# The last stage of an attention and gated feed-forward kernel as fifteen block products instead of seven, with some block sums made by adding transfers

## The chip, the cores and the metric

The kernel runs on one core of a Trainium2 chip. The metric is the device time of the program in microseconds (us). The core has a matrix engine (TensorE, PE in the rows; PEld is its weight load), a vector engine (DVE), a scalar engine (ACT), GpSimd (POOL) and a sync engine (SP) that issues most transfers; 16 DMA engines move the data. Each engine works through its own list of instructions in order, and waits where one of them needs something that isn't there yet.

## The reference

Eight sequences of 576 tokens with eight heads go through windowed attention. Its output is the input x of a gated feed-forward layer with 4608 tokens, 512 model channels and 1536 inner channels:

```
scores = where(mask, q @ k^T / 8 + bias, -1e9);  attn = softmax(scores)
x      = (attn @ v), heads put side by side            # [4608, 512]
hid    = sigmoid(x @ w_gate) * (x @ w_val)             # [4608, 1536]
out    = hid @ w_out                                   # [4608, 512]
```

This case is about the last line, out = hid @ w_out. In the kernel it is computed transposed: out^T, 512 rows by 4608 columns.

## The kernel before, in words

Three parts follow one another on the matrix engine: the attention (with the first feed-forward chunks beside it), then `ffn2`, which makes hid in chunks of 128 inner channels and writes them to DRAM, then `last`, which reads hid back and makes out. All three products of the feed-forward are in float32 quality: a value is split into a high part in the matrix engine's format (a cast) and the remainder (value minus high part, on the vector engine), and each product is three matmuls, high by high, high by remainder, remainder by high. A block of 128 by 1024 values costs one cast (scalar engine, or vector engine where the planner finds that better) and one subtraction of 1024 elements per partition on the vector engine. The function `parts` (lines 206 to 216 in its helpers `copy` and `minus`) issues the two.

`last` (called five times, from line 1068) works through five groups of columns, three of 2 x 512 and two of 2 x 384. In each group the product is cut 2 by 2 by 2: two halves of the output rows, two sets of six inner chunks, two halves of the columns. Seven block products, with sums of blocks ahead of them and sums of results behind them, take the place of eight. Block sums are made on the vector engine (line 881), results leave PSUM by the scalar engine (line 889) or are added there by the vector engine (line 892), and are stored by SP. The weight side of the seven products is made ahead by `prepare_o`, while `ffn2` runs: it decodes w_out, makes the sums, splits them into high part and remainder, and writes both to DRAM (`stash_o`). `fetch_o` reads them back into the places of the gate and value weights as `ffn2` gives these up. One product in a group is 36 matmuls: two row blocks, six inner chunks, three parts.

The split blocks ("duos", 128 x 1024, high part and remainder) lie in a ring of six buffers; a product uses three, so the next product can be prepared while one runs. The blocks of hid lie in fifteen places, twelve per group and three for sums.

The order of instructions on each engine is not written by hand: `Graph.order` plays the whole program with estimated costs (`dve_cost`, `act_cost`, transfer sizes over a rate) and each engine's list is the order that comes out. SP's list is one queue, in order: a load stands behind a store that waits for its result. For a vector instruction with two operands of 1024 elements `dve_cost` gives 1.13 us, for one that adds PSUM onto 512 elements 0.60 us.

## Time and profile before

| what | value |
|---|---|
| median of 3 runs | 962.1 us (962.04 to 962.5) |
| span of the profiled execution (the only time that its page gives) | 962.2 us |
| PE busy | 956.3 us, 99% |
| DVE busy | 763.7 us, 79% |
| ACT busy | 517.9 us, 54% |
| POOL busy | 143.7 us, 15% |
| moved by DMA | 186 MB, mean 193 GB/s, 56% of the 16 engines' time |

A row of the profile names an engine, a line of the kernel, the tile written and the tiles read, the shape, and the number of instructions; behind it stand the busy time, the mean of one instruction in ns, and how long the engine stood idle just before these instructions and for whom. Matmuls overlap, so that the mean ns of one is more than the time from one to the next. "Clock" is the TensorE clock that was granted, 1.00 being full speed.

### The profile page before, as it was taken

To read this page: it belongs to the slowest core of one execution; us is meant where nothing else is said; L and a number is where in the kernel's file an instruction comes from. 1 tells how busy PE (TensorE), PEld (TensorE's weight loads), DVE (VectorE), ACT (ScalarE), POOL (GpSimd) and SP (SyncE) were. 2 spreads that over 40 slices of the span, in tenths; PEclk is the share of its full clock that TensorE was granted. 3 is DMA by queue.
4 is the path that set the end of the run, shared out by engine and by line. 5 is a ranking of instruction groups with operands and counts; after the bars stand their busy time and mean duration, and the time that the engine had idled before them with its cause. 6 is when DMAs were issued, how large, how long until landed. Compare 5 with 4: busy or idle time off the path is not lost.

```text
span 962.2 us, 18740 instructions
## 1 busy us (share of the span) xinstructions
PE 956.3 (99%) x6648; PEld 834.5 (87%) x6648; DVE 763.7 (79%) x1893; ACT 517.9 (54%) x1341; POOL 143.7 (15%) x316
## 2 busy tenths in 40 slices
PE   8999999999999999999999999999999999999998
PEld 7778888888889999999988888888888888889998
DVE  7999788788898899878976775674598878878773
ACT  7998788878876354434533543443344433333341
POOL 3645345444441000000000000000000000000000
PEclk9999999999999999999999999999999999999999
DMA  8887678867654344335583483379856254352601
GB/s 295 274 280 256 223 266 291 282 203 241 232 198 162 122 147 138 104 143 191 179 287 113 159 284 132 143 284 347 317 189 204 103 166 163 94 167 91 189 25 50
DMA packets 82653, 186.03 MB, mean 193 GB/s; under 512 B 7808, under 2 KB 36864, under 8 KB 82560
## 3 DMA queue, kind: packets, MB, share of 16 engines
q1 hardware_dynamic: 82416, 184.71, 56.1%
q8 instruction: 52, 0.85, 0.4%
q14 instruction: 41, 0.34, 0.1%
q10 hardware_dynamic: 144, 0.13, 0.0%
HBM read 121.90 MB, written 62.91 MB: 192 GB/s over the span
## 4 chain that ended last, share of the span: by engine, by line
PE 98%; ACT 1%; DMA 1%; SPq 0%; DVE 0%; issue 0%; ACTq 0%
PE mm L795 42%; PE mm L929 27%; PE mm L661 14%; PE mm L461 5%; PE mm L532 4%; PE mm L575 3%; PE mm L613 2%; PE mm L292 1%; DMA early_ar<-in_q_dram 1%; ACT pb L490 0%; ACT early_h L207 0%; SPq L212 0%; DVE early_hs L680 0%; ACT cout L889 0%; ACT spread L207 0%
## 5 line engine op out<-in xcount | busy, mean ns | idle before, releaser
L795 PE MATMUL mm<-xc,w2s 128*128 128x384 f32 (+1 forms) x2016 | 404.0, 362 | 0.0
L795 PEld LDWEIGHTS mm<-xc,w2s 128*128 128x128 f32 x2016 | 363.7, 188 | 40.0 <-DVE later_hs L802 0.7
L929 PE MATMUL mm<-duo,wo 128*128 128x512 f32 (+1 forms) x1260 | 258.9, 367 | 0.0
L929 PEld LDWEIGHTS mm<-duo,wo 128*128 128x128 f32 x1260 | 229.3, 188 | 29.6
L661 PE MATMUL mm<-first,first 128*128 128x512 f32 x576 | 156.2, 407 | 0.1
L661 PEld LDWEIGHTS mm<-first,first 128*128 128x128 f32 x576 | 101.2, 188 | 21.3 <-issue 1.1
L806 ACT ACTIVATE sg<-mm 128x384 f32<-128x384 f32 (+1 forms) x96 | 52.2, 545 | 111.5 <-PE mm L795 63.3
L802 DVE TENSOR_TENSOR mm<-mm,low 128x384 f32<-128x384 f32 (+1 forms) x96 | 60.2, 628 | 61.1 <-PE mm L795 60.4
L207 ACT COPY low<-mm 128x512 f32<-128x512 f32 (+1 forms) x93 | 49.6, 536 | 77.8 <-PE mm L795 65.7
L490 ACT ACTIVATE pb<-pb,st 128x128 f32<-128x128 f32 x216 | 84.6, 398 | 2.0 <-DVE st L486 1.9
L586 POOL TENSOR_SCALAR_AFFINE_SELECT pt<-spread 128x384 f32<-128x384 f32 x96 | 53.1, 576 | 44.8 <-ACT spread L207 44.1
L586 POOL TENSOR_SCALAR_AFFINE_SELECT pt<-early_h 128x384 f32<-128x384 f32 x96 | 51.3, 553 | 56.4 <-ACT early_h L207 56.0
L478 DVE COPY_PREDICATED mm<-early_h,mm 128x256 f32<-128x256 int32 (+1 forms) x144 | 48.7, 388 | 5.8 <-PE mm L461 5.8
L532 PEld LDWEIGHTS mm<-pt,vr 64*64 64x64 f32 x1056 | 43.2, 133 | 10.0 <-issue 4.7
L486 DVE CUSTOM_DVE_ANT_0 pb<-mm,early_h 128x128 f32<-128x128 f32 x216 | 49.5, 281 | 0.0
L532 PE MATMUL mm<-pt,vr 64*64 64x192 f32 (+2 forms) x1056 | 47.3, 284 | 0.0
L568 DVE TENSOR_SCALAR pb<-pb,st 128x128 f32<-128x128 f32 x169 | 42.1, 295 | 1.3
L490 ACT ACTIVATION_READ_ACCUMULATOR pb<-pb,st 128x1 f32 x216 | 41.9, 194 | 0.0
L207 ACT CAST duo<-csum 128x1024 fp32r<-128x1024 f32 (+1 forms) x26 | 25.2, 970 | 30.2 <-PE mm L929 13.2
L810 DVE SCALAR_TENSOR_TENSOR later_hs<-sg,later_hs 128x384 f32<-128x384 f32 (+1 forms) x48 | 30.1, 626 | 13.8 <-ACT sg L806 13.6
L207 ACT COPY early_h<-mm 128x384 f32<-128x384 f32 (+3 forms) x75 | 32.1, 444 | 13.9 <-PE mm L532 8.7
L802 DVE TENSOR_TENSOR later_hs<-mm,later_hs 128x384 f32<-128x384 f32 (+1 forms) x48 | 29.7, 619 | 12.2 <-ACT sg L806 6.5
(144 smaller groups left out, 1204.9 us busy)
## 6 DMA issues: line engine op xcount, KB each, us to landing
hid<-later_hs SPq DMA_DIRECT2D x24, 512.0 KB, 3.4
wo<-stash_o SPq DMA_DIRECT2D x12, 896.0 KB, 7.6
vr<-in_v_dram SPq DMA_DIRECT2D x32, 288.0 KB, 4.7
hid<-later_hs SPq DMA_DIRECT2D x24, 384.0 KB, 2.9
stash_o<-wtmp SPq DMA_DIRECT2D x12, 768.0 KB, 3.9
wraw<-in_moe_w_gate_dram SPq DMA_DIRECT2D x14, 512.0 KB, 4.9
wraw<-in_moe_w_val_dram SPq DMA_DIRECT2D x14, 512.0 KB, 4.3
kr<-in_k_dram SPq DMA_DIRECT2D x11, 576.0 KB, 4.8
```

Of the source, the lines that this page charges most:

```text
L207: g.add("ACT", act_cost(n, psum), lambda: nc.scalar.copy(out(), src()), reads, writes, want, release=release, slack=slack, ways=[("DVE", d ...
L461: nc.tensor.matmul(to, qraw(u)[rows, i // 2, h * D:(h + 1) * D], keys, start=True, stop=True)
L478: g.add("DVE", dve_cost((a1 - a0) * P, psum=True), lambda b=b, a0=a0, a1=a1: nc.vector.copy_predicated(quads(b)[:, a0:a1, 1:3], before[:, ...
L486: g.add("DVE", 0.21, lambda: nc.vector.tensor_tensor_reduce(pb()[:, e], sp[b][:, a, D:D + P], relm[u.p][:, w], op0=ALU.add, op1=ALU.min, s ...
L490: g.add("ACT", 0.39, lambda: nc.scalar.activation(pb()[:, e], pb()[:, e], AF.Exp, bias=st()[:, e:e + 1], scale=-1.0, accum_out=st()[:, 3 + ...
L532: nc.tensor.matmul(mm[WORK[h]][e * D:(e + 1) * D, a - e * S - cuts[h]:b - e * S - cuts[h]], vraw(u)[r * D:r * D + D, c], seen, start=first ...
L586: nc.gpsimd.affine_select(pt(u)[:, f0:f0 + 2 * n - 1:2, :], both(), [[0, n], step], cmp, 0.0, base=0, channel_multiplier=mult)
L661: nc.tensor.matmul(mm[s][:, 0:wd], w.tile(kind, wi, i)[:, c * P:(c + 1) * P], xpart(x, c)[:, 0:wd], start=(k == 0 and c == 0), stop=(k == ...
L795: nc.tensor.matmul(mm[b][:, 0:N2], w.tile2(i, wp)[:, wk, c * P:(c + 1) * P], combo(k, xp, N2)[:, c], start=(start and c == 0 and j == 0), ...
L802: g.add("DVE", dve_cost(N2, psum=True), lambda: nc.vector.tensor_tensor(o(), bk(b)(), a(), op=ALU.add), [("mm", b), *reads] if okeys else ...
L806: g.add("ACT", act_cost(N2, psum=True), lambda: nc.scalar.activation(sg[h](), bk(b)(), AF.Tanh, scale=0.5), [("mm", b)], [("sg", h)], F)
L929: nc.tensor.matmul(mm[b][:, 0:N2], wo2(2 * q + m, wp)[:, k, j * P:(j + 1) * P], duo(xp)[:, m], start=(k in (0, 3, 1) and q == 0 and m == 0 ...
```

## The change

The last stage is cut 2 by 3 by 3: two halves of the output rows (256 each), three thirds of the inner channels (four chunks each), and three blocks of 512 columns, so that there are three calls of `last`, each for 1536 columns. Fifteen block products stand in the place of eighteen. One product is 24 matmuls of 512 columns (two row blocks, four inner chunks, three parts).

hid lies in DRAM as [128, 2, 512] for each third, pair of chunks and column block, so that `ffn2` stores a chunk's two halves with two or three transfers (`put`) instead of one. A load in `last` is one such block, 512 KB with 4 KB per partition. Sixteen blocks of two pairs are loaded per call, and five more (`more`) are added by the transfer itself onto a block already loaded: GpSimd issues a DMA with an add. Ten sums per call are made on the vector engine (`sums`). Results go through `snap` (scalar engine), `plus` and `both` (vector engine).

Weights: `prepare_o` runs four times instead of six, and makes eleven sums of 256 columns each time, for most of which only the sum itself is stored; `fetch_o` reads these six tiles of 896 KB and splits them after loading, on the scalar and the vector engine. The other four tiles (`LATER`) come with both parts. Two of the ring's places and two others now hold these weights: the ring has four duos instead of six, and the blocks of hid have eleven places. The start and step of the weights' preparation in the planner (`OUT0`, `OSTEP`) go from 430 and 36 to 425 and 48.

```diff
-OUT0, OSTEP = 430.0, 36.0
+OUT0, OSTEP = 425.0, 48.0
...
+SLOTS = (1, 2, 0, 3, 4, 5)
+LATER = (("w2s6", "w2", 14), ("h3", "moe", 6), (f"ar{HOME[5]}", "moe", 8), (f"ar{HOME[2]}", "moe", 8))
...
+ORDER = (11, 6, 13, 7, 12, 8, 5, 14, 10, 2, 1, 0, 3, 9, 4)
+RANK = {p: i for i, p in enumerate(ORDER)}
+ADD, SUB = ALU.add, ALU.subtract
+BATCHES = (((6, (0, 0), ADD, (0, 2)), (7, 6, SUB, (1, 0)), (8, (1, 2), SUB, 7)),
+           ((11, (1, 1), ADD, (1, 2)), (13, 11, SUB, (0, 1)), (12, (0, 2), SUB, 13)),
+           ((0, (0, 0), ADD, (0, 1)), (1, (0, 0), SUB, (1, 0)), (3, (0, 1), ADD, (1, 0))),
+           ((4, (1, 1), SUB, (0, 1)), (9, (1, 0), ADD, (1, 1))))
+SINGLES = ((10, (1, 0)), (2, (0, 1)), (5, (0, 2)), (14, (1, 2)))
...
-    stash_o = [dram.tile([2, P, 7 * 2 * P], F32, name=f"stash_o{i}") for i in range(NFC // 2)]
-    hid = {(c, q, t): dram.tile([2, P, 2 * n2], F32, name=f"hid{c}{q}{t}")
-           for c in range(2) for q in range(NDUO) for t, (_, n2) in enumerate(GROUPS)}
+    stash_o = [dram.tile([P, 7, 2 * P], F32, name=f"sums_o{z}") for z in range(len(SLOTS))]
+    stash_o += [dram.tile([P, n, 2 * P], F32, name=f"parts_o{z}") for z, (_, _, n) in enumerate(LATER)]
+    hid = {(k, q, t): dram.tile([P, 2, NB], F32, name=f"hid{k}{q}{t}")
+           for k in range(3) for q in range(2) for t in range(NB9)}
...
+    def put(fc, a, b, src, keys, F):
+        while a < b:
+            t = a // NB
+            e = min((t + 1) * NB, b)
+            move(lambda t=t, a=a, e=e: hid[fc // 4, fc // 2 % 2, t][:, fc % 2, a - t * NB:e - t * NB],
+                 lambda a=a, e=e: src(a, e), keys, [("hid", fc, t, a)], F, (e - a) / 2, True)
+            a = e
...
+    def prepare_o(kt, want, release):
...
+        decode(wo, kt, gt, kg, want, release)
+        for k in (1, 2):
+            decode(wo, 4 * k + kt, lambda k=k: tt()[:, 2 * k - 2:2 * k].rearrange("p a f -> p (a f)").bitcast(I32), kt0, want, release + step / 3 * k)
...
+            for o, (p, a, op, b) in enumerate(batch):
+                va, vb, vo = val(a), val(b), val(p)
+                g.add("DVE", dve_cost(2 * P, two=True), lambda va=va, vb=vb, vo=vo, op=op: nc.vector.tensor_tensor(vo(), va(), vb(), op=op),
+                      [key(a), key(b)], [("wtmp", z, o)], want, port=True, release=release + (n + 1) * step)
...
+                hi, lo, v = (lambda o=o, z=z: six(z)[:, o, 0]), (lambda o=o, z=z: six(z)[:, o, 1]), val(p)
+                g.add("ACT", act_cost(2 * P), lambda hi=hi, v=v: nc.scalar.copy(hi(), v()), [("wtmp", z, o)], [("wtmp", z, "hi", o)], want)
+                g.add("DVE", dve_cost(2 * P, two=True), lambda hi=hi, lo=lo, v=v: nc.vector.tensor_tensor(lo(), v(), as32(hi()), op=SUB),
+                      [("wtmp", z, "hi", o)], [("wtmp", z, o)], want, port=True)
+                move(lambda y=y, i=i: stash_o[y][:, i:i + 2], lambda z=z, o=o: as32(six(z))[:, o], [("wtmp", z, o), ("wtmp", z, "hi", o)],
+                     [("stash_o", y, i)], want, 256)
...
+    def fetch_o(z):
+        F, keys = FIRST + 1.5, [("stash_o", z, i) for i in range(14)]
+        if z < len(SLOTS):
+            old = [[("w2", SLOTS[z], p, a) for a in (0, 2)] for p in range(2)]
+            move(lambda: as32(wo2(z, 1)), lambda: stash_o[z], keys, [("wo", z, 1), *old[1]], F, 896, True)
+            g.add("ACT", act_cost(14 * P), lambda: nc.scalar.copy(wo2(z, 0), as32(wo2(z, 1))), [("wo", z, 1)], [("wo", z, 0), *old[0]], F)
+            g.add("DVE", dve_cost(14 * P, two=True), lambda: nc.vector.tensor_tensor(wo2(z, 1), as32(wo2(z, 1)), as32(wo2(z, 0)), op=SUB),
+                  [("wo", z, 0)], [("wo", z, 1)], F, port=True)
+            return
...
+        move(lambda: as32(wo2(z)), lambda: stash_o[z], keys, [("wo", z, 0), *old], F + 0.5, 128 * n, True)
...
-            c, q, m = place(fc)
-            move(lambda: hid[c, q, t][m].rearrange("p (h t) -> p h t", h=2), lambda: hs(e)[:, :, 0:N2], [kp, kv], [("hid", fc, t, 0)], F, N2, True)
+            for h in range(2):
+                put(fc, t0 + h * N2, t0 + (h + 1) * N2, lambda a, b, h=h: hs(e)[:, h, a - t0 - h * N2:b - t0 - h * N2], [kp if h else kv], F)
...
-    RING = (0, 3, 4, 1, 5, 2)
+    RING = (0, 3, 4, 1)
     ducks = [0]
+    stage_free = [("xr", i) for i in range(4)] + [("wraw0", 0), ("wraw1", 0), ("tt", 0), ("hs0", 0), ("hs1", 0)] + [(f"ar{HOME[6]}", i) for i in range(2)]
+    SHAPES = {"xr": 4, "wraw0": 1, "wraw1": 1, "tt": 1, "hs0": 1, "hs1": 1, f"ar{HOME[6]}": 2}
+    post_free = [("sg0", 0), ("sg1", 0), ("wbits0", 0), ("wbits1", 0), ("tt", 2)] + [(h, i) for h in ("h4", "h2") for i in range(4)]
...
+        def load(name, k, n):
+            slots = [stage_free.pop(0) for _ in range(2)]
+            rows[name] = slots
+            for q, slot in enumerate(slots):
+                move(lambda slot=slot: staged(slot), lambda q=q: hid[k, q, 3 * t + n], hid_keys(k, n, q), [("row", *slot)], F, 512, True)
...
+        def more(name, k, n):
+            for q, slot in enumerate(rows[name]):
+                g.add("POOL", 1.2, lambda slot=slot, q=q: nc.gpsimd.dma_start(staged(slot), hid[k, q, 3 * t + n], accum_op=ALU.add),
+                      hid_keys(k, n, q), [("row", *slot)], F, size=512 / 300.0, port=False)
+
+        def sums(o, a, b, op):
+            for q in range(2):
+                so, sa, sb = rows[o][q], rows[a][q], rows[b][q]
+                g.add("DVE", dve_cost(2 * NB, two=True), lambda so=so, sa=sa, sb=sb: nc.vector.tensor_tensor(staged(so), staged(sa), staged(sb), op=op),
+                      [("row", *sa), ("row", *sb)], [("row", *so)], F, port=True)
...
+        def snap(name, chain, j):
+            keep_at((name, j))
+            b = bks[chain, j]
+            o = val((name, j))
+            g.add("ACT", act_cost(NB, psum=True), lambda: nc.scalar.mul(o(), mm[b], 0.5), [("mm", b)], [key((name, j))], F)
...
+        def plus(o, chain, a, j, scale=0.5):
+            b, va = bks[chain, j], val((a, j))
+            g.add("DVE", dve_cost(NB, psum=True), lambda: nc.vector.scalar_tensor_tensor(va(), mm[b], scale, va(), op0=ALU.mult, op1=ALU.add),
+                  [("mm", b)], [key((a, j))], F)
...
+            for q in range(2):
+                slot = rows[name][q]
                 r = RING[ducks[0] % len(RING)]
                 ducks[0] += 1
-                duo = lambda p, r=r: T(moe, f"duo{r}", [P, 2, 2, NB], F32R, tag=f"ar{HOME[r]}")[:, p, :, 0:N2]
-                parts(lambda duo=duo: duo(0), lambda duo=duo: duo(1), val, n, [key], ("ar", r, 0), ("ar", r, 1), F)
+                duo = lambda part_, r=r: T(moe, f"duo{r}", [P, 2, 2, NB], F32R, tag=f"ar{HOME[r]}")[:, part_]
+                hi, lo, v = (lambda duo=duo: duo(0)), (lambda duo=duo: duo(1)), (lambda slot=slot: staged(slot))
+                copy(hi, v, 2 * NB, [("row", *slot)], [("ar", r, 0)], F)
+                minus(lo, v, lambda hi=hi: as32(hi()), 2 * NB, [("row", *slot), ("ar", r, 0)], [("ar", r, 1)], F, pool=False)
...
+                start = (chain, j) not in bks
+                if start:
+                    bks[chain, j] = bank()
+                b = bks[chain, j]
...
+                then(j)
+
+        add, sub = ALU.add, ALU.subtract
+        load("10", 1, 0)
+        product(11, "A", "10", lambda j: snap("a1", "A", j))
+        load("00", 0, 0)
+        product(6, "B", "00", lambda j: snap("b1", "B", j))
+        load("21", 2, 1)
+        sums("10", "21", "10", sub)
+        product(13, "A", "10", lambda j: snap("a2", "A", j))
+        drop("10")
+        load("22", 2, 2)
+        sums("00", "22", "00", sub)
+        product(7, "B", "00", lambda j: snap("b2", "B", j))
+        drop("00")
+        product(12, "A", "21", lambda j: snap("a3", "A", j))
+        drop("21")
+        product(8, "B", "22", lambda j: snap("b3", "B", j))
+        drop("22")
+        load("20", 2, 0)
+        load("f", 0, 0)
+        more("f", 2, 1)
+        sums("f", "20", "f", sub)
+        product(5, "A", "f", lambda j: (plus("y00", "A", "b1", j), store("y00", 0, 0, j)))
+        drop("f")
+        load("g", 1, 0)
+        more("g", 2, 2)
+        sums("g", "20", "g", sub)
+        drop("20")
+        product(14, "B", "g", lambda j: (plus("y10", "B", "a1", j), store("y10", 1, 0, j)))
+        drop("g")
+        load("02", 0, 2)
+        load("i", 0, 0)
+        more("i", 1, 2)
+        sums("i", "02", "i", sub)
+        product(10, "C", "i", lambda j: plus("y12", "C", "b3", j))
+        drop("i")
...
+        for z in range(len(SLOTS), len(SLOTS) + len(LATER)) if t == 0 else ():
+            fetch_o(z)
...
+        def zero(j):
+            plus("dd", "D", "d1", j)
+            both("y01", "a3", "dd", add, j)
+            store("y01", 0, 1, j)
+            both("y02", "y02", "dd", sub, j)
+            free("dd", j)
+        product(0, "D", "01", zero)
...
+        load("k", 1, 1)
+        more("k", 1, 2)
+        load("21", 2, 1)
+        sums("k", "k", "21", sub)
+        drop("12", "21")
+        product(4, "F", "k", lambda j: (plus("y11", "F", "a2", j), store("y11", 1, 1, j)))
+        drop("k")
...
-    for n in range(NFC // 2):
-        prepare_o(n, 2.0e6 + n, OUT0 + OSTEP * n)
+    follow([("wtmp", z, *y) for z in range(2) for o in range(3) for y in ((o,), ("hi", o))])
+    for kt in range(KC):
+        prepare_o(kt, 2.0e6 + kt, OUT0 + OSTEP * kt)
...
-    for n in range(NFC // 2):
-        fetch_o(n)
-    raws_at = lambda z0, z1: [("raw", *y) for y, z in RAW.items() if z0 <= z < z1]
-    follow(later_xr + raws_at(0, 4))
-    follow([("w2", 6, p, a) for p in range(2) for a in (0, 2)] + raws_at(4, 7))
+    for z in range(len(SLOTS)):
+        fetch_o(z)
```

On the vector engine, before, in the first group of the last stage; duo is a split block, csum a sum of blocks, cout a result:

```order
L881 TENSOR_TENSOR rows_xr<-rows_xr,csum_6910 128x1024
L216 TENSOR_TENSOR duo_7338<-csum_6974,duo_7338 128x1024
L881 TENSOR_TENSOR csum_6936<-csum_6936,rows_xr 128x1024
L892 SCALAR_TENSOR_TENSOR cout_7427<-mm_78,csmall_7377 128x512
L881 TENSOR_TENSOR csum_6974<-csum_6974,rows_xr 128x1024
L216 TENSOR_TENSOR duo_7288<-csum_6910,duo_7288 128x1024
L881 TENSOR_TENSOR rows_hs_7228<-rows_hs_7228,csum_6936 128x1024
L892 SCALAR_TENSOR_TENSOR cout_7454<-mm_75,csmall_7403 128x512
L216 TENSOR_TENSOR duo_7299<-csum_6936,duo_7299 128x1024
L216 TENSOR_TENSOR duo_7309<-csum_6974,duo_7309 128x1024
L881 TENSOR_TENSOR rows_hs_7266<-rows_hs_7266,csum_6974 128x1024
```

After, in the first call of `last`, around the eighth and ninth product; rows are blocks of hid and their sums (in place), part is a result:

```order
L230 TENSOR_TENSOR duo_7499<-rows_xr,duo_7499 128x1024
L230 TENSOR_TENSOR duo_7502<-rows_xr,duo_7502 128x1024
L970 SCALAR_TENSOR_TENSOR part_wbits_7579<-mm_73,part_wbits_7579 128x512
L942 TENSOR_TENSOR rows_wraw_6844<-rows_xr,rows_wraw_6844 128x1024
L970 SCALAR_TENSOR_TENSOR part_wbits_7598<-mm_74,part_wbits_7598 128x512
L230 TENSOR_TENSOR duo_7456<-rows_wraw_6844,duo_7456 128x1024
L970 SCALAR_TENSOR_TENSOR part_sg_7543<-mm_75,part_sg_7543 128x512
L942 TENSOR_TENSOR rows_tt<-rows_wraw_6792,rows_tt 128x1024
L970 SCALAR_TENSOR_TENSOR part_sg_7561<-mm_76,part_sg_7561 128x512
L942 TENSOR_TENSOR rows_xr<-rows_ar_7520,rows_xr 128x1024
L230 TENSOR_TENSOR duo_7466<-rows_tt,duo_7466 128x1024
L942 TENSOR_TENSOR rows_hs_7359<-rows_xr,rows_hs_7359 128x1024
```

Beside four remainders (written to duo) there stood five sums and two results; now there stand four sums and four results.

On GpSimd, before, the last three rows, which make weight sums (tt, wbits, wg) during `ffn2`:

```order
L215 TENSOR_TENSOR tt<-wbits_422 128x256
L215 TENSOR_TENSOR tt<-tt 128x256 x2
L215 TENSOR_TENSOR wg_5665<-wbits_422,wg_5665 128x256 x3
```

After, the first five of thirty rows in the last stage, each a transfer that adds a block of hid onto a loaded one:

```order
L936 DMA rows_ar_7520<-hid_158 128x1024
L936 DMA rows_xr<-hid_167 128x1024
L936 DMA rows_xr<-hid_159 128x1024
L936 DMA rows_xr<-hid_168 128x1024
L936 DMA rows_wraw_6844<-hid_141 128x1024
```

GpSimd had nothing to do in the last stage, and now issues two transfers for each of five sums in each call.

On SP, before, the loads of the second and third group among the stores of results:

```order
L212 DMA rows_w2s_7349<-hid_138 128x2x512
L212 DMA out_dram<-cout_7454 128x512
L212 DMA rows_w2s_7349<-hid_143 128x2x512
L212 DMA out_dram<-cout_7427 128x512
L212 DMA out_dram<-cout_7454 128x512
L212 DMA out_dram<-cout_7427 128x512
L212 DMA out_dram<-cout_7454 128x512
L212 DMA rows_xr<-hid_119 128x2x512
L212 DMA rows_xr<-hid_124 128x2x512
```

After, the seam between `ffn2` and the last stage; wo are weights, parts_o and hid lie in DRAM:

```order
L226 DMA rows_ar_7520<-hid_166 128x1024
L226 DMA rows_ar_7520<-hid_121 128x1024
L226 DMA wo_w2s_7531<-parts_o_117 128x3584
L226 DMA hid_171<-later_hs_7223 128x512
L226 DMA hid_170<-later_hs_7223 128x512
L226 DMA rows_xr<-hid_130 128x1024
L226 DMA rows_xr<-hid_139 128x1024
L226 DMA rows_xr<-hid_148 128x1024
L226 DMA rows_xr<-hid_123 128x1024
```

The loads of the first sums (rows_xr) stand behind a weight tile of 1792 KB and the last two stores of `ffn2`.

## Rows read from the trace of the kernel before

**Rows 1.** The chain that ended last, 690 to 962: start, length, engine and line.
```profile
689.84 10.36 PE mm L795 x45
700.20 258.77 PE mm L929 x1260
958.96 0.02 issue
958.99 0.49 ACT cout L889
```

**Rows 2.** Stretches of the last stage: length, busy time by engine, clock, DMA share, GB/s.
```profile
core 0: us, PE busy (x) PEld busy (x) DVE busy (x) ACT busy (x) POOL busy (x), PEclk, DMA share, GB/s
704.00:804.00 100.00, 100.00 (x443) 82.81 (x442) 81.75 (x78) 39.74 (x45) 0.00 (x0) 1.00 0.52 168
704.00:854.00 150.00, 150.00 (x664) 124.19 (x663) 121.62 (x116) 59.57 (x68) 0.00 (x0) 1.00 0.47 150
700.00:959.00 259.00, 258.95 (x1261) 229.12 (x1259) 201.98 (x215) 95.76 (x119) 0.00 (x0) 1.00 0.41 130
```

**Rows 3.** Matmuls of line 929 by shape: count, busy us, mean ns, idle before.
```profile
L929 PE MATMUL mm<-duo,wo 128*128 128x512 f32 x756 | 171.5, 389 | 0.0
L929 PE MATMUL mm<-duo,wo 128*128 128x384 f32 x504 | 87.6, 334 | 0.0
```

**Rows 4.** The vector engine by line and shape, 700 to 962: count, busy, mean, idle before.
```profile
L216 DVE TENSOR_TENSOR duo<-rows_hs,duo 128x1024 fp32r<-128x1024 f32 x12 | 14.5, 1219 | 3.8 <-ACT duo L207 3.8
...
L881 DVE TENSOR_TENSOR csum<-csum,rows_xr 128x1024 f32<-128x1024 f32 x9 | 11.0, 1218 | 0.1
...
L892 DVE SCALAR_TENSOR_TENSOR cout<-mm,csmall 128x512 f32<-128x512 f32 x12 | 8.2, 683 | 0.2 <-PE mm L929 0.2
...
L881 DVE TENSOR_TENSOR csum<-csum,rows_xr 128x768 f32<-128x768 f32 x6 | 5.7, 952 | 0.1
...
L208 DVE CAST duo<-rows_xr 128x1024 fp32r<-128x1024 f32 x3 | 2.1, 694 | 5.2 <-PE mm L929 5.2
```

**Rows 5.** Waits of the vector engine, 700 to 962: total us, times, longest.
```profile
DVE duo L208 <- PE mm L929: 21.9, 19, 2.4
DVE duo L216 <- ACT duo L207: 12.3, 24, 0.8
DVE cout L892 <- PE mm L929: 9.6, 8, 2.6
DVE csum L881 <- DMA rows_w2s<-hid: 5.0, 6, 1.5
```

**Rows 6.** The busiest stretches of the vector engine under a full TensorE, columns as Rows 2.
```profile
340.00:380.00 40.00, 40.00 (x231) 39.83 (x231) 37.89 (x65) 21.75 (x42) 1.48 (x2) 1.00 0.44 142
700.00:720.00 20.00, 20.00 (x90) 16.53 (x89) 19.22 (x20) 7.07 (x8) 0.00 (x0) 1.00 0.51 160
```

**Rows 7.** Transfers issued 700 to 962: queue totals, then kind, count, size, median us to landing.
```profile
q1 hardware_dynamic: 19779, 33.56, 40.0%
...
out_dram<-cout SPq DMA_DIRECT2D x24, 256.0 KB, 2.7
...
out_dram<-cout SPq DMA_DIRECT2D x16, 192.0 KB, 1.9
```

**Rows 8.** Transfers 646 to 655, the most loaded stretch: packets and their queue.
```profile
DMA packets 1131, 3.67 MB, mean 408 GB/s; under 512 B 97, under 2 KB 225, under 8 KB 1131
...
q1 hardware_dynamic: 1131, 3.67, 103.4%
```

**Rows 9.** All transfers that read or write hid, 690 to 962: landing time.
```profile
DMA to landing us min/median/max: 3.0/4.0/8.4
```

**Rows 10.** Transfers issued 600 to 700, columns as Rows 7.
```profile
hid<-later_hs SPq DMA_DIRECT2D x10, 512.0 KB, 8.2
...
rows_xr<-hid SPq DMA_DIRECT2D x4, 512.0 KB, 5.7
...
csum<-hid SPq DMA_DIRECT2D x3, 512.0 KB, 10.5
```

**Rows 11.** Groups of the stage in which the weights are made, 440 to 660, columns as Rows 4.
```profile
L216 DVE TENSOR_TENSOR wtmp<-tt,wtmp 128x1536 fp32r<-128x1536 f32 x6 | 10.5, 1752 | 0.1
...
L216 DVE TENSOR_TENSOR tt<-tt,wbits 128x256 f32<-128x256 f32 x5 | 2.1, 419 | 0.0
```

**Rows 12.** Four stretches before the last stage, columns as Rows 2.
```profile
460.00:500.00 40.00, 40.00 (x193) 35.02 (x192) 35.95 (x49) 18.67 (x30) 1.89 (x2) 1.00 0.74 266
540.00:580.00 40.00, 40.00 (x178) 33.08 (x177) 32.31 (x44) 20.02 (x31) 1.02 (x1) 1.00 0.67 237
620.00:660.00 40.00, 40.00 (x178) 33.05 (x177) 27.28 (x39) 19.10 (x29) 1.23 (x1) 1.00 0.75 291
660.00:700.00 40.00, 40.00 (x177) 32.94 (x176) 21.41 (x29) 15.52 (x24) 0.00 (x0) 1.00 0.87 312
```

More of the change, by code (lines that the diff above doesn't have):

```diff
@@ L711, in prepare2, with at_o, unit @@
                   [k, *pool], ("w2", i, 0, a), ("w2", i, 1, a), want)
[L713 to L714 removed]
+    NWHOLE = 7 * len(SLOTS)
+    pairs = [(len(SLOTS) + z, i) for z, (_, _, n) in enumerate(LATER) for i in range(0, n, 2)]
+    def at_o(p, kt):
+        n = 4 * RANK[p] + kt
+        return divmod(n, 7) if n < NWHOLE else pairs[n - NWHOLE]
+    def unit(p, kt, part_):
+        z, i = at_o(p, kt)
+        return (z, i, part_) if z < len(SLOTS) else (z, i + part_, 0)
@@ L876, in last @@
-        x = {(h, c, q): (lambda h=h, c=c, q=q: raw2(h, c, q, N2)) for h, c, q in RAW}
-        kx = {y: ("raw", *y) for y in RAW}
-        def add(o, a, b, op, reads, writes):
-            way = ("POOL", 0.1 + n * 0.00223, True, lambda: nc.gpsimd.tensor_tensor(o(), a(), b(), op=op))
-            g.add("DVE", dve_cost(n, two=True), lambda: nc.vector.tensor_tensor(o(), a(), b(), op=op), reads, writes, F, port=True, ways=[way])
-        bks = [[bank() for _ in range(3)] for _ in range(2)]
-        bk = lambda b: (lambda: mm[b][:, 0:N2])
@@ new lines, in six @@
+                                nc.tensor.matmul(mm[b], wo2(z, part_)[:, i, j * P:(j + 1) * P], duo(xp)[:, m],
+                                                 start=start and q == 0 and m == 0 and e == 0, stop=q == 1 and m == 1 and e == 2, skip_group_check=True)
+                    g.add("PE", 6 * (NB / 2400 + 0.0133), six, [("ar", r, 0), ("ar", r, 1)] + sorted({("wo", z, part_) for z, _, part_ in units.values()}),
+                          [("mm", b), *(["seam"] if t == 0 and p == ORDER[0] else [])], 1.0e6)
@@ new lines, in last @@
+        product(14, "B", "g", lambda j: (plus("y10", "B", "a1", j), store("y10", 1, 0, j)))
[6 more added lines that the diff above has]
+        drop("i")
+        load("j", 0, 1)
+        more("j", 1, 0)
+        load("11", 1, 1)
+        sums("j", "11", "j", sub)
+        drop("11")
+        product(2, "F", "j", lambda j: snap("d1", "F", j))
@@ new lines, in last @@
+        drop("j")
+        for z in range(len(SLOTS), len(SLOTS) + len(LATER)) if t == 0 else ():
+            fetch_o(z)
+        load("01", 0, 1)
+        load("22", 2, 2)
+        sums("02", "01", "02", add)
+        sums("02", "02", "22", sub)
+        drop("22")
+        product(1, "C", "02", lambda j: plus("y02", "C", "b2", j))
+        drop("02")
+        def zero(j):
[4 more added lines that the diff above has]
+            free("dd", j)
@@ new lines, in last @@
+        product(0, "D", "01", zero)
+        load("12", 1, 2)
+        sums("01", "01", "12", add)
+        product(3, "F", "01", lambda j: (plus("y02", "F", "y02", j), store("y02", 0, 2, j)))
+        drop("01")
+        product(9, "E", "12", lambda j: (plus("y12", "E", "y12", j), store("y12", 1, 2, j), plus("a2", "E", "a2", j, -0.5)))
+        load("k", 1, 1)
[4 more added lines that the diff above has]
+        product(4, "F", "k", lambda j: (plus("y11", "F", "a2", j), store("y11", 1, 1, j)))
```

200 lines of the change are left out of this document (81 added, 119 removed).

## The prediction

> **What bounds the kernel now.** I read the chain of waits first: from 700.2 to 959.0 us nothing but matmuls of line 929 stands on it, 258.8 us of 1260 matmuls, then 0.5 us of the scalar engine and the last store up to 962.2 [rows 1]. So the last stage is bound by the matrix engine, without a gap, at clock 1.00 [rows 2]. The stretches say how near the others are: over the stage the vector engine is busy 202.0 of 259.0 us (78%), the scalar engine 95.8, the DMA engines 41% [rows 2]. From the groups of the vector engine, and then from the transfers, I took durations by shape.
>
> **The matrix engine.** Matmuls of 512 columns take 171.5/756 = 0.227 us each, those of 384 columns 87.6/504 = 0.174 [rows 3]; between 804 and 854 us 664 - 443 = 221 start in 50 us, 0.226 each [rows 2]. After: 3 calls x 15 products x 24 = 1080 matmuls of 512 columns, 1080 x 0.2268 = 244.9 us. Against 258.8 that is -13.9 us; nothing else in the path of the stage is taken away. One product lasts 5.44 us, one call 81.6.
>
> **The vector engine in the last stage.** From the order of the changed kernel: 90 remainders at 1.219, 60 sums at 1.218, 54 results added from PSUM at 0.685, 21 casts at 0.694 [rows 4], and 12 sums of 512 elements that the trace doesn't show; from 1024 elements in 1.218 and 768 in 0.952 [rows 4] I get 0.69. The sum is 109.7 + 73.1 + 37.0 + 14.6 + 8.3 = 242.7 us. So its load goes from 78% to 242.7/244.9 = 99%. The planner's own figures (1.13 and 0.60) are lower by 7 and 12%, so its order leaves less room than it counts on.
>
> The work is spread evenly. A split block goes into a ring of four, so that the seventh product of a call can be split only when the fifth has given its first duo up, three quarters through: 4.75 x 5.44 = 25.8 us after the call began. From there to the first remainder of the fifteenth product the order of the first call has 17 remainders, 15 sums, 12 results, 4 small sums and 3 casts, 52.0 us: ready at 77.8, wanted at 14 x 5.44 = 76.2. In the second and third call it is 12 sums and 4 casts, 49.1 us: ready at 74.9. Without any wait the vector engine thus costs the matrix engine 1.6 us once. Every wait of it beyond some 1 us per call comes on top. In the stage before it waited 21.9 us for matmuls and 12.3 for casts [rows 5]; of these, the waits for matmuls go when it is late itself, those for casts partly.
>
> How busy can it be with no gap in the matrix engine? The trace shows 19.22 of 20 us, 96%, and 37.89 of 40, 95% [rows 6]. I take 96%: 242.7/0.96 = 252.8 us, 7.9 us more than the matmuls. Bounds: 1.6 us (no waits); at 94%, somewhat below the 95% row, 258.2, 13.3 us.
>
> **Transfers in the last stage.** One call loads 32 blocks of 512 KB (16.8 MB), adds 10 (5.2 MB), stores 12 results of 256 KB (3.1 MB): 25.2 MB in 81.6 us, 309 GB/s, where the stage before moved 130 [rows 2]. The rate at full load lies between 33.56 MB in 40.0% of 262 us, 320 GB/s, with rows of 2 KB [rows 7] and 408 GB/s [rows 8]. By these a call's transfers take 62 to 79 us of 81.6 if adding costs no more than loading. What an adding transfer takes no row shows: none is issued by GpSimd in the stage before. Below, it is a load, 3.0 us at the least and 4.0 in the middle [rows 9]; above, twice the slowest load, 16.8. I take 6 us, once and a half the middle.
>
> The time there is for it: take the second block of the sum for the ninth product. Its place comes free with a remainder of the sixth product, and the sum stands sixteen vector instructions further on; between them lie 6 remainders, 4 sums, 3 results and 2 casts, 15.6 us. In these the load is issued and lands (4.0; 5.7 where the queue is full [rows 10]), GpSimd sees it and issues the add, and this lands: 4.0 + 6 or 5.7 + 6 and a gap of a us or two, 11 to 14 us. It fits, with little to spare; so I put nothing on it beyond the 4% above.
>
> On who carries the bytes, the trace has only transfers of the one hardware queue [rows 7]. The Trainium skill, "DMA: Bandwidth & Descriptors", section "Issuing engines are not separate DMA queues", says that transfers from different engines run on the same 16 engines and interleave. By it the adds take part in the 25.2 MB, as counted; if they had engines of their own, 20.0 MB would be left, 49 to 62 us. Either fits under the matmuls.
>
> **The rest.** The weights: 62 vector instructions of 256 elements (0.42 us) and six of 1792 (near the 1.75 of 1536) in place of 30 and six [rows 11], some 14 us more over stretches in which the vector engine is busy 21 to 36 of 40 us under a full matrix engine [rows 12]. Cost 0, with -0.5 and +2 as bounds: without that cover the subtraction of a fetched tile stands in front of the last chunks' results. Stores of hid: 120 transfers in place of 48, off any path. Weights fetched at the seam: 4.7 MB more in the first call, less in the stretch ahead; 0 to +3 us. The end: the last result goes through a vector instruction of 0.69 in place of 0.49 us, and a store of 256 KB in place of 192 KB, 2.7 against 1.9 us [rows 1, 7]: +1.0.
>
> **Sum**, against the span of 962.2 (median of the runs 962.1, so the two are one): 962.2 - 13.9 + 7.9 + 1.0 = 957.2 us. Its own range is 950 to 963.
>
> **Rivals.**
> 1. All of the gain arrives: the waits of the vector engine stay within the 1.6 us. 962.2 - 13.9 + 1.6 + 1.0 = 950.9. For it: the even spread, and places that come free early. Against: no row shows more than 96%.
> 2. The adding transfers come late, and the kernel gets slower. The place is the sum behind each add; the price decides from an add of some 9 us, where 5.7 + 9 + 1 passes 15.6. For it: rows of hid landed in 5.7 to 10.5 us where the queue was full [rows 10], and the queue will be 76 to 97% full. With an add of 12 us each of the five sums of a call is 3 us late; since the next add is under way meanwhile I count two of five, 6 us a call, 18 in all, on top of the 7.9: 962.2 - 13.9 + 7.9 + 18 + 1.0 = 975.2. Against: the rate of 408 GB/s leaves a quarter of the time free. The Trainium skill, "DMA: Bandwidth & Descriptors", section "Rules for kernel authors", says that an accumulating transfer reads its destination and writes it later. By it 30.4 MB pass in a call, 75 to 95 us of 81.6, and this rival holds; no run so far shows it.
> 3. The vector engine simply can't be kept at 96% and settles at 94%: 962.2 - 13.9 + 13.3 + 1.0 = 962.6, no change. For it: 12.3 us of waits for casts in the stage before, and two fewer duos in the ring.
>
> **Chances.** Forecast 0.42, rival 1 0.14, rival 2 0.28, rival 3 0.16. Below 960.2 (0.2%, about what a measurement of this kernel can tell) lie rival 1, nearly all of the forecast and a little of rival 3: faster 0.57. Within 0.2%: 0.12, from rival 3 and the edges of the forecast. Slower: 0.31, rival 2 and the rest of rival 3. The range reaches from 949, just below rival 1, to 979, past rival 2.
>
> **What would show it.** The matmuls of the stage: 1080, in some 245 us plus gaps; gaps named for remainders on the vector engine are the forecast, for sums that wait for a transfer rival 2. The vector engine's groups should sum to 243 us. The adds' time to landing decides: 6 us or less speaks for the forecast, 9 or more for rival 2. Gaps ahead of 700 us would say that the weights were costed wrongly. I am wrong if the stage takes under 246 us or over 262.

## The result and the profile after

The change made the kernel slower: 976.4 us (975.49 to 977.6, 4 runs) against 962.3 on the same chip, ratio 1.0143, 95% interval [1.0129, 1.0157]. 957.2 had been forecast. The profiled execution spans 975.1 us.

The matrix engine's stretches, answering to [rows 2]; one row for about one call of `last`, which is 360 matmuls, 81.6 us without a gap:

```profile
core 0: us, PE busy (x) PEld busy (x) DVE busy (x) ACT busy (x) POOL busy (x), PEclk, DMA share, GB/s
700.00:797.00 97.00, 88.66 (x370) 71.65 (x369) 79.23 (x84) 33.70 (x40) 9.75 (x11) 0.95 0.97 317
797.00:887.00 90.00, 85.67 (x371) 68.81 (x370) 77.02 (x82) 33.08 (x39) 9.03 (x10) 1.00 0.95 285
887.00:972.00 85.00, 78.11 (x337) 62.35 (x335) 67.19 (x73) 26.02 (x31) 7.85 (x9) 1.00 0.75 223
```

The matrix engine, without a gap before, now idles 8.3, 4.3 and 6.9 us; 1.3 of the last figure lie behind the last matmul, so the waits are 18.1 us. The stage is longer by more than that: 27.3 us over its matmuls without a gap, 13.4, 6.2 and 7.6 by calls of 360 matmuls. Of the 9.2 us that are no waits, 4.4 are matmuls at a lower granted clock behind two waits of the first call (shown in the last section). The DMA engines are busy 95% and 97% in two calls, at 285 and 317 GB/s. Whom the matrix engine waits for, and whom the vector engine (answering to [rows 5]; total us, times, longest):

```profile
PE mm L1011 <- DVE duo L230: 18.1, 12, 5.0
```
```profile
DVE rows_xr L942 <- DMA rows_xr<-hid: 14.2, 6, 5.4
DVE rows_tt L942 <- DMA rows_tt<-hid: 11.2, 2, 6.0
DVE rows_xr L942 <- DMA rows_ar<-hid: 5.0, 1, 5.0
DVE rows_wraw L942 <- DMA rows_wraw<-hid: 4.8, 1, 4.8
...
DVE rows_ar L942 <- DMA rows_ar<-hid: 1.9, 2, 1.5
```

The gaps are named for remainders (L230), but the vector engine comes to those late because its sums (L942) stood some 38 us waiting for transfers, 33 for adding ones and 5.0 (the third line) for a plain load; the longest wait of a sum for a transfer was 1.5 us in [rows 5]. The transfers, answering to [rows 7] and [rows 9]: queue totals, a load (SPq) and an adding transfer (POOLq) with the median us to landing, then the landing of all thirty adding transfers:

```profile
q1 hardware_dynamic: 19009, 61.71, 58.8%
q0 software_dynamic: 4320, 15.73, 28.7%
...
rows_xr<-hid SPq DMA_DIRECT2D x31, 512.0 KB, 6.6
...
rows_xr<-hid POOLq DMA_DIRECT2D x8, 512.0 KB, 9.1
```
```profile
DMA to landing us min/median/max: 5.4/9.3/13.7
```

An adding transfer lands after 9.3 us where 6 had been taken, and its bytes occupy the DMA engines longer: 28.7/15.73 against 58.8/61.71 per MB, 1.9 times. The chain of waits, answering to [rows 1], shows where this stands on the path (start, length; a piece of the second call):

```profile
801.12 1.23 DVE duo L230
802.35 0.02 issue
802.37 4.27 DMA rows_xr<-hid
...
807.26 9.06 DMA rows_xr<-hid
...
816.35 0.04 DVE rows_xr L942
...
817.49 1.22 DVE duo L230
...
823.42 1.24 DVE duo L230
824.66 0.02 issue
824.68 8.20 DMA rows_hs<-hid
...
833.50 10.82 DMA rows_hs<-hid
...
844.34 1.23 DVE rows_hs L942
```

Read it downwards: a remainder gives a place up (802.35), the load into it takes 4.27 us, GpSimd issues the add at 807.26, that takes 9.06, the sum can start at 816.35. From place to sum 14.0 us, and 19.7 the second time. The first and the third call, transfers of the chain alone:

```profile
708.44 13.42 DMA rows_xr<-hid
723.49 13.73 DMA rows_xr<-hid
...
738.49 13.81 DMA rows_ar<-hid
...
891.63 4.84 DMA rows_ar<-hid
897.10 8.18 DMA rows_ar<-hid
907.69 5.23 DMA rows_xr<-hid
913.54 8.97 DMA rows_xr<-hid
```

The third call has the same pair twice, 13.7 and 14.8 us from place to sum; the first has one of 28.8 us, in which the load alone takes 13.42 beside the weights and other loads. What follows it in the first call, at 738.49, is no adding transfer but a plain load of 13.81 us; the sum that waits for it stands before the matrix engine's longest wait, 5.0 us. It runs beside adding transfers, which from 735 to 745 us take 70.0% of the DMA engines' time (q0) for about half of the bytes:

```profile
q0 software_dynamic: 383, 1.40, 70.0%
q1 hardware_dynamic: 375, 1.36, 36.1%
```

### The profile page after: what moved, and what is told of

It is laid out like the page before. It is cut to its first block, busy times and chain, and to the rows that moved or that the text cites. A ratio compares the mean times of both kernels' runs of the same rounds, so it can differ in the third digit from the quotient of the medians.

```text
span 975.1 us, 18738 instructions
## 1 busy us (share of the span) xinstructions
PE 950.1 (97%) x6468; PEld 808.7 (83%) x6468; DVE 794.8 (82%) x1947; ACT 526.6 (54%) x1348; POOL 162.5 (17%) x337
## 3 DMA queue, kind: packets, MB, share of 16 engines
q0 software_dynamic: 4320, 15.73, 8.4%
## 4 chain that ended last, share of the span: by engine, by line
PE 75%; DMA 11%; DVE 9%; issue 3%; ACT 1%; POOL 0%; DVEq 0%; POOLq 0%; ACTq 0%
PE mm L850 40%; PE mm L681 14%; DMA rows_xr<-hid 6%; PE mm L1011 6%; PE mm L476 5%; DVE duo L230 4%; PE mm L547 4%; PE mm L590 3%; DMA rows_ar<-hid 3%; DMA rows_hs<-hid 2%; PE mm L628 2%; DVE rows_xr L942 1%; PE mm L307 1%; DVE part_h L970 1%; DVE rows_hs L942 1%
## 5 line engine op out<-in xcount | busy, mean ns | idle before, releaser
L1011 PE MATMUL mm<-duo,wo 128*128 128x512 f32 x756 | 180.7, 398 | 18.1 <-DVE duo L230 18.1
L1011 PEld LDWEIGHTS mm<-duo,wo 128*128 128x128 f32 x756 | 143.6, 191 | 54.3 <-DVE duo L230 24.2
L936 POOL DMA_DIRECT2D rows_ar<-hid x7 | 6.3, 897 | 375.2 <-DMA rows_ar<-hid 375.2
L221 ACT CAST duo<-rows_xr 128x1024 fp32r<-128x1024 f32 x29 | 30.4, 1053 | 36.0 <-DVE rows_xr L942 25.8
L230 DVE TENSOR_TENSOR duo<-rows_xr,duo 128x1024 fp32r<-128x1024 f32 x35 | 42.5, 1222 | 0.8 <-ACT duo L221 0.5
```

The costliest lines, as they stand in the source:

```text
L221: g.add("ACT", act_cost(n, psum), lambda: nc.scalar.copy(out(), src()), reads, writes, want, release=release, slack=slack, ways=[("DVE", d ...
L230: g.add("DVE", dve_cost(n, psum, True), lambda: nc.vector.tensor_tensor(out(), a(), b(), op=ALU.subtract), reads, writes, want, port=not p ...
L1011: nc.tensor.matmul(mm[b], wo2(z, part_)[:, i, j * P:(j + 1) * P], duo(xp)[:, m], start=start and q == 0 and m == 0 and e == 0, stop=q == 1 ...
```

## The experiments

Theories at the start: A, the adding transfer is dear (slow to land, about twice a load's time on the DMA engines); B, two transfers one behind the other into few places are too long a chain, whatever the second one does; C, the vector engine is full and adding has nothing to do with it. Each kernel is an edit of the changed one, with its ratio to the seven products; the edits are shown shortened. Runs 1 to 3 and 8 to 10 keep the changed kernel's order of instructions. In the others the planner makes a new order, which can move the time by itself (run 4).

**1. No adding transfers**; five operands of each call lack a term.

```diff
-  lambda ...: nc.gpsimd.dma_start(staged(slot), hid[k, q, 3 * t + n], accum_op=ALU.add)
+  lambda slot=slot, q=q: None
```

> Leaves out the thirty adding transfers (five blocks per call are not added); every other instruction and its order stay. Theory A (an adding transfer costs the DMA engines about twice a load, lands late, and slows the loads beside it): the gaps of the matrix engine in the last stage go from 26 us to 2 to 8, so 951 to 958 us. Theory B (not the price of the add, but the chain of two transfers through few places): the chain is gone too, so also 951 to 958. Theory C (the vector engine, 99% full, is what stops the matrix engine): its work is unchanged, 970 or more.

953.0 us, 0.9900 [0.9872, 0.9929], the whole forecast gain and more. C falls: with nearly the same 242 us of vector work the matrix engine waited once, 2.7 us, in the first call.

**2. The same transfers without the add**: GpSimd issues them, they overwrite the place.

```diff
-  nc.gpsimd.dma_start(staged(slot), hid[k, q, 3 * t + n], accum_op=ALU.add)
+  nc.gpsimd.dma_start(staged(slot), hid[k, q, 3 * t + n])
```

> The same thirty transfers from the same engine at the same places and with the same bytes from DRAM, but they overwrite instead of adding (the five sums per call lack the first block). Theory A: near the run without them, at most 4 us more, 953 to 961. Theory B: the chain load, wait, second transfer, sum is as long in links as before, so 970 to 977. Theory C: 970 or more.

959.1 us, 0.9960 [0.9948, 0.9972]. Of the 23.4 us between run 1 and the changed kernel, 6.1 are for a second transfer at all, 17.3 for its adding (4.9 and 17.6 in the last stage of the traces). B as the whole cause falls. Its adds' landing and its chain:

```profile
DMA to landing us min/median/max: 3.7/6.7/9.6
```
```profile
796.61 4.82 DMA rows_xr<-hid
...
802.07 6.67 DMA rows_xr<-hid
...
808.76 0.03 DVE rows_xr L942
...
811.15 5.59 DMA rows_tt<-hid
...
817.38 6.58 DMA rows_tt<-hid
...
823.98 0.04 DVE rows_tt L942
```

The same pairs at the same point, 12.1 and 12.8 us from place to sum (11.0 and 12.7 in the third call), and none in the first. Calls two and three have 62.2 us of such windows with adding, 48.6 without; these are 13.6 us longer, the two calls themselves 8.9. The first call is 8.7 us longer; there the plain load of 13.8 us lands after 9.4 without the adding. So A holds. In the later calls it works by the chain of B, in the first call also by the loads beside the adds. The run takes the adds' longer landing and their longer hold on the DMA engines away together (28.7% to 15.0% for the same 15.73 MB), and doesn't part the two.

**3. No sums on the vector engine** (L942), adding transfers kept; the operands lack those terms.

```diff
-  lambda ...: nc.vector.tensor_tensor(staged(so), staged(sa), staged(sb), op=op)
+  lambda so=so, sa=sa, sb=sb: None
```

> Leaves out the sixty sums on the vector engine (products take the loaded blocks, or the blocks with an add, as they are); all transfers stay. The vector engine has 73 us less to do, 169 of 245. Theory C: the gaps go, 950 to 954. Theories A and B: the casts of the blocks with an add now wait for the transfer that the sums waited for; part of the gaps stays, 960 to 974.

957.7 us, 0.9949 [0.9927, 0.9972]: between the theories. The adds land as late as ever, and the DMA engines are fuller than in the changed kernel, yet the matrix engine is busy 89.48 of 90 us in the second call:

```profile
DMA to landing us min/median/max: 5.7/9.5/14.2
```
```profile
700.00:797.00 97.00, 92.17 (x399) 74.02 (x398) 60.48 (x66) 36.44 (x43) 10.03 (x11) 1.00 1.00 330
797.00:887.00 90.00, 89.48 (x394) 73.49 (x394) 57.93 (x64) 35.60 (x42) 10.79 (x12) 1.00 0.96 299
```

So late adds and full DMA engines alone make little of the loss (the stage is some 4 us longer than run 1's): the sums have a part in it, by their work or because they stand on the chain between the add and the cast.

**4. The order, with the engines' measured times** in the planner.

```diff
-  dve_cost(2 * NB, two=True) ... dve_cost(NB, psum=True) ... act_cost(NB, psum=True) ... size=512 / 300.0
+  1.22 ... 0.69 ... 0.6 ... size=2 * 512 / 400.0
```

> Only the planner's prices for the last stage are set to what the trace of the changed kernel shows (two-block instructions on the vector engine 1.22 us, one-block ones 0.69 us, scalar-engine copies 1.05 and 0.6 us, an adding transfer twice the bytes of a load); the work is the same, only its order moves. Theory O (the order is made with a price for the adding transfers that is too low, and a better order hides them): 958 to 967 us. Theory A (the adding transfers fill the DMA engines, and no order hides that): 972 to 980 us.

973.4 us, 1.0110 [1.0089, 1.0132]. Some 3 us of the 23.

**5. All casts of blocks on the scalar engine.**

```diff
-  copy(hi, v, 2 * NB, [("row", *slot)], [("ar", r, 0)], F)
+  g.add("ACT", act_cost(2 * NB), lambda ...: nc.scalar.copy(hi(), v()), [("row", *slot)], [("ar", r, 0)], F)
```

> The casts of the blocks that the planner put on the vector engine (21 of the 84, 0.69 to 0.73 us each, 15 us in all) all go to the scalar engine, which is busy 93 us of the stage. Theory A+C (late adding transfers cost so much because the vector engine, full, cannot catch up): 962 to 970 us. Theory A alone (the transfers' price and nothing on the vector engine): 974 to 978 us.

979.4 us, 1.0175 [1.0153, 1.0196], above both: 14.7 us less vector work made nothing better. That the amount of work is without effect doesn't follow, since a cast on the scalar engine takes 1.05 us, on the vector engine 0.70, and stands on the same chain, in a new order. The matrix engine's waits for remainders fell from 18.1 to 10.9 us, and one of 7.3 us for a cast came up. That cast stood behind a sum that had waited 7.15 us for the first call's plain load, here 14.2 us.

**6. Fewer adding transfers.** Operands of the fifth and the fourteenth product from sums that are in memory: 12 adds and 12 loads less, 12 sums more.

```diff
-  load("f", 0, 0); more("f", 2, 1); sums("f", "20", "f", sub); product(5, "A", "f", ...)
-  load("g", 1, 0); more("g", 2, 2); sums("g", "20", "g", sub); product(14, "B", "g", ...)
+  sums("20", "20", "21", sub); sums("20", "20", "22", sub)
+  sums("00", "20", "00", add); product(5, "A", "00", ...)
+  sums("10", "20", "10", add); product(14, "B", "10", ...)
```

> The operands of the two products of the third block column of rows are made from sums already in memory: 4 of the 10 adding transfers of a call and the 4 loads beneath them go (12 of 30 in all), and 4 sums of 1.22 us of the vector engine a call come in their place (14.6 us in all). Theory A (what counts is adding transfers, 23 us for 30): 965 to 969 us. Theory C (what counts is the vector engine's 223 of 272 us): 980 us or more. Theory A+C: in between, 968 to 978 us.

961.6 us, 0.9994 [0.9983, 1.0004]. 14.8 us back, though the vector engine has 14.0 us more of sums (and 11 casts less, 247.4 us in all against 242.5). That is more than any theory said, and it speaks for the transfers; but the edit also takes two chains and their places out of each call. In the traces the stage is 16.3 us shorter, 9.7 of them waits; the granted clock, 0.995 on average in the changed kernel, is 1.000 here. Waits of the matrix engine:

```profile
PE mm L1011 <- DVE duo L230: 8.5, 8, 2.5
```

**7. Runs 4 to 6 together**, by the three edits above.

> The three changes together: 12 of 30 adding transfers less, all casts of blocks on the scalar engine, measured prices in the plan. Theories A and A+C: 952 to 959 us, under the seven products' 962.3. Theory C alone: 970 us or more, since the vector engine's sum of work stays the same (14.6 us more, 15 us less).

962.0 us, 0.9993 [0.9979, 1.0007]: no better than run 6 alone.

**8. The wait moved, the work kept.** Sums behind an adding transfer work on the other operand, in place.

```diff
-  sums("f", "20", "f", sub)    # and g, i, j, k
+  tensor_tensor(20, 20, 20) in its place of the order; the cast reads f
```

> The 30 sums that read what an adding transfer made are worked, at the same places of the vector engine's order, on the other operand in place; the casts then read the added block itself. The vector engine's work is the same to the instruction, the transfers too; only the sums no longer wait for adding transfers, the casts do (in the output these five operands lack one term). Theory W (the price comes in through the vector engine standing in order before a sum whose adding transfer is late): 957 to 966 us. Theory L (what counts is that transfers and vector work are both near full, wherever the wait stands): 970 to 978 us.

969.7 us, 1.0075 [1.0061, 1.0090].

**9. The waits kept, half of the sums' work gone.**

```diff
-  nc.vector.tensor_tensor(...)      # sums of 10, 00, 02 (two), 01
+  None
```

> The other half: the 30 sums of 1.22 us that read no adding transfer's block emit nothing (36.6 us less of the vector engine's work; in the output these operands are one block instead of a sum), the 30 that wait for adding transfers stay. Theory W: 968 to 976 us. Theory L: 962 to 968 us, half of what leaving out all 60 sums gave (18.7 us).

968.2 us, 1.0059 [1.0045, 1.0073]. Neither W nor L alone: run 8 gives 6.7 us back, run 9 8.2, and leaving all sums out (run 3) 18.7. By calls, run 8 is 13.5, 2.8 and 5.3 us over 81.6 (13.4, 6.2 and 7.6 in the changed kernel): moving the wait helped the later calls and not the first, where a sum waits 6.2 us for the plain load, here 18.1 us.

**10. Short stores.**

```diff
-  move(lambda: out[r:r + P, c:c + NB], v, ...)
+  move(lambda: out[r:r + P, c:c + 64], lambda: v()[:, 0:64], ...)
```

> Each store of a finished block of the output writes 64 of its 512 columns (32 KB in place of 256 KB; some 8 MB less of traffic in the stage, as much as 16 loads; the output's other columns stay unwritten). Everything else is the same in the same order. If an adding transfer is late because the DMA engines are nearly full: its landing falls from 9.3 us and the time to 962 to 972 us. If it is late by itself: landing stays above 8.5 us and the time at 973 to 978 us.

977.9 us, 1.0163 [1.0150, 1.0177]: nothing. Loads land sooner (6.6 to 5.2 us), adding transfers do not:

```profile
rows_xr<-hid SPq DMA_DIRECT2D x31, 512.0 KB, 5.2
...
rows_xr<-hid POOLq DMA_DIRECT2D x8, 512.0 KB, 8.9
```

The DMA engines stayed 94% busy in the first call, so this doesn't empty the queue, and fullness isn't excluded. That an adding transfer is mostly late of itself has run 6 for it: its DMA engines are busy 77% of the stage (90% in the changed kernel), and its 18 adds still land after 8.6 us.

**11. The 1792 KB of weights later**, behind the add of the seventh operand.

```diff
-  F, keys = FIRST + 1.5, [("stash_o", z, i) for i in range(14)]
+  F, keys = FIRST + 1.5, [("stash_o", z, i) for i in range(14)] + [("row", *slot) for slot in rows["i"]]   # first tile of LATER
```

> The transfer of 1792 KB of weights that stands in SP's queue at the beginning of the stage (issued at 699.7 us, landed 15.8 us later, first read at 767.5) is issued only after the adding transfer for the seventh operand of the first call. If the first call's extra loss over the later ones (12.1 us against 6.0 and 8.4) is the weights' share of the DMA engines: 969 to 973 us. If not: 974 to 979 us.

974.5 us, 1.0132 [1.0119, 1.0145]: 2 us, too little to tell from none. By calls the matrix engine takes 8.6, 7.4 and 8.1 us over 81.6, where it was 13.4, 6.2 and 7.6 (12.1, 6.0 and 8.4 as the expectation counts). So the first call's extra loss does go with the later weights, but the two other calls, in a new order, lose 1.7 us more; this run doesn't settle it.

**12. The order, with measured landings**: as run 4, and an add lands 4.5 us, a load 2.2 us later in the plan.

```diff
-  hid_keys(k, n, q), [("row", *slot)], F, size=512 / 300.0, port=False)
+  hid_keys(k, n, q), [("row", *slot)], F, size=2 * 512 / 400.0, port=False, margin=4.5)
```

> Only the order moves: the planner takes the measured times of the vector and scalar engines in the last stage, an adding transfer as landing 4.5 us later than it did (near the 9.3 us measured, where it had counted with about 4) and a load 2.2 us later, so that it no longer puts a sum ahead of remainders that are ready earlier. If the loss is the order, made with landings that are too early: 960 to 969 us. If landings that late leave no good order: 970 to 977 us.

972.9 us, 1.0119 [1.0105, 1.0133]. The sums' waits for transfers fall from 38 us to 6.4, and the matrix engine still waits:

```profile
DVE rows_xr L942 <- DMA rows_xr<-hid: 4.9, 2, 3.9
...
DVE rows_hs L942 <- DMA rows_hs<-hid: 1.5, 1, 1.5
```
```profile
PE mm L1011 <- DVE duo L997: 14.6, 11, 2.8
```

So the vector engine standing before late sums is not the whole loss: with this chain of places neither order that the planner found hides the adds.

**13. Six more adding transfers as loads and sums**, on run 6 with run 4's prices, and run 6 with the prices alone.

```diff
-  more("j", 1, 0)
+  load("t", 1, 0); sums("j", "j", "t", add); drop("t")
```

> As the run before it, with 6 more of the remaining 18 adding transfers replaced by a load to a place of its own and a sum of 1.22 us on the vector engine (7.3 us more of its work). Theory A (adding transfers count, 0.8 us each): 953 to 957 us. Theory L: 957 to 963 us, what the transfers give the vector engine takes.

> The version with 12 adding transfers and 12 loads less (961.6 us), with the planner's prices set to the measured ones, the casts left where the planner puts them. By the 3 us that the prices gave alone: 957 to 960 us, under the seven products' 962.2. If prices and fewer transfers repair the same thing: 960 to 963 us.

965.6 us, 1.0038 [1.0022, 1.0053], and 964.2, 1.0021 [1.0010, 1.0031]. Below 18 adds nothing more comes back. Whether the 7.3 us of further sums take it, no run shows; and run 4's prices, which gave 3 us on the changed kernel, lose 2.6 on run 6.

**14. Run 6 with the casts on the scalar engine** (the edit of run 5), **and with late weights** (that of run 11).

> The version with 12 adding transfers and 12 loads less (961.6 us), with all casts of blocks on the scalar engine. If the vector engine is what bounds that version (its waits for adding transfers are 18 us now): 957 to 960 us, under the seven products' 962. If not: 961 to 965 us.

> The version with 12 adding transfers and 12 loads less (961.6 us), with the same late transfer of the weights. If the seam's traffic still costs there: 958 to 961 us; if not: 961 to 964 us.

961.7 us, 0.9995 [0.9986, 1.0003], and 966.5, 1.0049 [1.0037, 1.0060]: no gain, and a loss. Nor did run 12's prices and landings and the casts together help it:

> The same version with measured times of the engines, the later landings and all casts of blocks on the scalar engine (12 to 15 us less of the vector engine's work). If order and vector engine are what is left: 955 to 960 us. If not: 961 to 966 us.

965.0 us, 1.0034 [1.0021, 1.0047], with 241 us of vector work.

**15. Run 6 with measured landings only.**

```diff
-  ..., [("row", *slot)], F, 512, True)          # load
+  ..., [("row", *slot)], F, 512, True, margin=2.2)
-  ..., F, size=512 / 300.0, port=False)         # more
+  ..., F, size=2 * 512 / 400.0, port=False, margin=4.5)
```

> The version with 12 adding transfers and 12 loads less (961.6 us), with the same later landings in the plan (times of the engines left as they were). If its 18 us of waits of the vector engine come from the order: 956 to 960 us, under the seven products' 962. If not: 961 to 966 us.

959.5 us, 0.9973 [0.9961, 0.9985]: faster than both kernels, by 2.2 us against the seven products, and this with 254.2 us of vector work, the planner having put the casts there again. Waits of the matrix engine:

```profile
PE mm L1011 <- DVE duo L230: 5.7, 5, 1.5
PE mm L1011 <- ACT duo L221: 0.6, 2, 0.3
```

## Why the prediction was wrong

**The step that failed** is "Transfers in the last stage": "I take 6 us", "It fits, with little to spare; so I put nothing on it". The add landed after 9.3 us, within the bounds of 3.0 and 16.8 but past the point of 9 us at which rival 2 was to decide. The place was right, the sum behind the add; the windows on the chain measured 13.7 to 19.7 us in the later calls, against 11 to 14 forecast and 15.6 of cover. That cover counted vector work as if it were always there to hide behind. The plain second transfer, with windows of 11.0 to 12.8 us in the later calls, already made these two calls 4.9 us longer than without it, so the true cover was shorter. The step also took 4.0 to 5.7 us for a load; in the first call two loads took 13.4 and 13.8.

**The sum, term by term**, in spans of profiled executions. Matrix engine -13.9: right, run 1 shows 1080 matmuls and no gap but one. The stage's matmuls begin at 698.5 instead of 700.0 us, where 0 (-0.5 to +2) was put for the weights; but runs 1, 2, 3 and 10, the same kernel up to there, begin at 697.7 to 701.8, so the 1.5 us can't be called theirs. The last matmul ends 4.35 us before the end of the span, before 3.2: +1.1 (forecast +1.0). Between lie 272.2 us, 27.3 more than the 244.9 of the matmuls, where 7.9 was put. Run 1 splits them: its stage takes 249.7 us, so 4.8 are there without adding transfers (one wait for the vector engine, 2.7, and slower matmuls), and 22.5 come with them, where 0 was put. The vector engine's tally was right: 242.5 us, summed over its groups, against 242.7 forecast; over run 1's stage that is 97% in place of 96%. 962.2 - 1.5 + (272.2 - 258.9) + 1.1 = 975.1.

**The rivals.** Rival 2 held, with 975.2 us and, in the later calls, with its mechanism; the size was partly luck, since it counted 7.9 + 18 for vector engine and adds where 4.8 + 22.5 came, had the loss come from an add of 12 us, and knew neither the slow plain load nor the lower clock of the first call. It said for itself that the DMA engines would be 76 to 97% full. They were, but run 3, at 100 and 96% in two calls, is 4.7 us above run 1, so fullness and late adds without the sums cost little of the 23.4. The Trainium skill, "DMA: Bandwidth & Descriptors", section "Rules for kernel authors", says that an accumulating transfer reads its destination and writes it later. The trace agrees with counting its bytes twice, as the prediction did by that rule: 1.9 times the engine time per MB, and 0.97 times once the add is left out (run 2). Rival 1's time, 950.9 us, is near run 1's span of 951.5, without adds, but with 4.8 us of loss where it had 1.6. Rival 3 (94%) didn't come.

**What stays open.** The amount of vector work alone doesn't decide: 226.6 us of it with the casts gone (run 5) is no faster than 242.5, and 254.2 (run 15) is the fastest version that leaves nothing out. But run 9 gave 8.2 us for 36.7 us of sums less. That the sums matter because they lengthen the chain from a place to its next use fits runs 3, 5, 8, 9 and 15, but no run changed that chain alone, with more places. Nor did any part an add's late landing from its hold on the DMA engines, or measure an adding transfer with nothing else moving.

## What to carry to other kernels

An adding transfer is not a load with a sum for free: count its landing (here 9.3 us against 5.7 to 7.7 for loads) on the chain from a place given up to the next use, and look at how many places that chain has to lie in. Vector work between the ends of a chain is not cover to be counted in full. Count also what an adding transfer does to the loads beside it. Better prices in the planner are no steady gain: measured landings gave 2 us on the version with fewer adds, while measured times of the engines gave 3 us on the changed kernel and lost 2.6 on that version.

## What the hardware showed besides

After the matrix engine's longest idle time in the stage, 5.0 us, the granted clock fell to 0.5 (the 1.2 GHz level) as it began again (columns as in the first block):

```profile
747.00:751.40 4.40, 2.73 (x13) 1.91 (x11) 0.32 (x1) 0.86 (x1) 0.00 (x0) 1.00 1.04 297
751.40:754.80 3.40, 0.07 (x1) 0.07 (x1) 2.48 (x3) 0.00 (x0) 0.00 (x0) 0.85 1.03 408
754.80:758.00 3.20, 3.20 (x8) 2.55 (x9) 3.20 (x4) 1.05 (x1) 0.00 (x0) 0.50 1.03 373
```

Eight matmuls in 3.2 us, where 14 pass at 0.227. The matmuls behind the two longest waits of the first call, up to the next wait each (start, length, count and the wait before them):

```profile
739.65 10.08 PE L1011 MATMUL mm<-duo,wo 128*128 128x512 f32 x36 [2.28 <-DVE duo L230]
754.73 5.49 PE L1011 MATMUL mm<-duo,wo 128*128 128x512 f32 x12 [5.01 <-DVE duo L230]
```

At 0.227 from one to the next and 0.389 for the last they take 8.3 and 2.9 us, so 1.8 and 2.6 us, 4.4 in all, went to the clock. Not every such wait does this: behind the longest one of run 6, 2.53 us, 76 matmuls take 17.5 us at clock 1.00, 0.1 more than that count. And an adding transfer holds GpSimd for 0.87 us each, a plain one 0.53.
